# Linear attention and a gated feed-forward on one core: Silu as tanh and a product during the attention

## The chip, the cores and the metric

The kernel runs on one core of one Trainium2 chip. The metric is the time of one execution in microseconds (us) on the device. A core has TensorE (PE: matrix products and transposes, into the accumulator memory PSUM), VectorE (DVE), ScalarE (ACT: functions such as exp, and copies), GpSimd (POOL) and SyncE (SP, which here issues the DMAs). Each engine runs its own instructions in the order of its queue; semaphores order the engines among each other.

## The reference

Eight batches of eight heads, 576 tokens, head dimension 64, 128 random features, all in float32; then a gated feed-forward part on 4608 tokens of 512 numbers with 1536 hidden units.

```python
def phi(x):
    proj = einsum('bhsd,md->bhsm', x, omega)
    sq = sum(x * x, axis=-1, keepdims=True) / 2.0
    h = proj - sq
    h = h - max(h, axis=-1, keepdims=True)
    return exp(h) / sqrt(m)
q_p, k_p = phi(q * scale), phi(k * scale)
kv = einsum('bhsm,bhsd->bhmd', k_p, v)
z = sum(k_p, axis=2)
attn = einsum('bhsm,bhmd->bhsd', q_p, kv) / (einsum('bhsm,bhm->bhs', q_p, z)[..., None] + 1e-06)
x = attn.transpose(0, 2, 1, 3).reshape(4608, 512)
g = x @ w_gate
out = (g * (1.0 / (1.0 + exp(-g))) * (x @ w_val)) @ w_out
```

## The kernel before

Two streams of work share the engines for the first half of the time: the attention, and the feed-forward part of the tokens that are already through it.

**The attention** goes in steps. A step takes two groups of 256 tokens of a pair of heads, first keys alone, then a query and a key group each, at the end two query groups. For a step PE transposes q and k (the tile pt, copied to x by ACT, L454), PE projects them (pp, L469), DVE takes the maxima (L490) and forms the bias (L492, L493), and ACT takes Exp into ph (L505). POOL makes the squares (L446). The keys' ph go into the running sums kvacc on PE; ACT copies a finished sum out (kvr, L521). A query's ph is transposed on PE (ptq) and copied by ACT into a tile qt (`q_transpose`, L632 and L633). For the first four batches the quotient comes after the product with kv: PE makes po (`q_mult`), DVE divides (xn, L658), PE transposes xn (xt). For the later four the quotient comes first: POOL multiplies ph by the sums of the keys (jk, L563 and L567), DVE adds up and inverts (dj, L571 to L573), POOL scales ph (L583), and the matmuls of `q_out` make xt from qt and kvr. ACT copies xt into the resident tiles of the first three token tiles (L709, with DVE's L710 for the low part), or into xo, which a DMA stores for later (L703, L704).

**The feed-forward part.** Tokens come in nine tiles of 512, the hidden units in twelve blocks of 128. Each operand is split into a high and a low part, and a product is three matmuls. In the first round three token tiles (0 to 2) meet four sets of three blocks: twelve visits, in the generator `stream`. A visit makes for each block f of its set the gate g (twelve matmuls into one PSUM bank of the pool of three that `ps_moe` hands out), then Silu of each gate on ACT into the SBUF tile sl (L800), then the products of the visit before with w_out that are still due (`down`), then for each block the value v (twelve matmuls), h = v times sl on DVE (L820), and the split of h by ACT (L823) and POOL (L824). `down` adds its results up in acc, by ACT's copy the first time (L760), by DVE after that (L763). The weights are converted on the way by ACT, DVE and POOL (L289 to L303) and split by L263 and L264. In the second half, after the attention, the six other token tiles are taken in pairs by a scheme with seven products (`pair_rounds`), with a Silu of its own (L1038), which the change leaves alone.

**What orders the work.** The steps' functions are called in a written order (`CLOSE`, then `GROUPED`); between them the function `give` draws from `stream` as much matrix work as a plan of due times says. The framework then places the instructions of every engine from this order, their dependences and the free buffers. After the last step the attention's pools are closed (`late.close()`), and the dictionary `late_pools` gets the pools of the second half; until then it is empty. Eleven of the twelve visits have issued their Silus by then; the twelfth visit's three come after it. `att` is one of the attention's pools; with bufs=N a tile of a tag waits until the N-th one before it has been read for the last time.

Of the kernel before, what the change touches and what calls it, by code (L numbers as in the profile page):

```python
# [11 lines left out]
F32 = mybir.dt.float32  # L12
# [4 lines left out]
AF = mybir.ActivationFunctionType  # L17
ALU = mybir.AluOpType
# [6 lines left out]
def kernel(  # L25
# [11 lines left out]
    nc = tc.nc  # L37
# [4 lines left out]
    P = 128  # L42
# [5 lines left out]
    G = 256  # L48
    CH = G // P
    T = 512  # L50
# [40 lines left out]
    att = late.enter_context(tc.tile_pool(name="att", bufs=2))  # L91
# [14 lines left out]
    def transpose(*args, **kw):  # L106
        newest_pe[:] = [nc.tensor.transpose(*args, **kw)]  # L107
        return newest_pe[0]
# [10 lines left out]
    def ps_moe(name, shape):  # L119
        return ps_m.tile(shape, F32, name=name, tag="m")  # L120
# [21 lines left out]
    def slots(n, kind):  # L142

        if not 0 <= n < NS:
            return []
        return [(i, b, g, (kgroups if kd == "k" else qgroups)[g]) for i, (kd, b, g) in enumerate(steps[n]) if kd == kind]
# [25 lines left out]
    def mm1_us(w):  # L172
        return 3 * NC * (w / 2.4 + 13) * US
# [31 lines left out]
    for n in range(NN + 1):  # L205
        vi = 0
# [111 lines left out]
    def need(f, i):  # L318
        while (f, i) not in converted:
            tick()  # L320
# [4 lines left out]
    def load_weights(f, i):  # L325
        need(f, i)
        landing.append([LAND, f, i, fetch((f,), i)[0]])

    def land(upto=None):

        for t in landing:
            t[0] -= upto is None
        while landing and (landing[0][0] <= 0 or upto in [(f, i) for _, f, i, _ in landing]):
            _, f, i, raw = landing.pop(0)
            new_weights(f, i)
            with behind_step():
                split_piece(f, i, raw)

    def fetch(fs, i, spare=None):
        raws_ = []  # L340
        for f in fs:
            if spare is None:
                raw = moe.tile([P, DM], F32, name=f"wraw{f}_{i}", tag="wraw", bufs=3)
            else:
                raw = spare.tile([P, DM], F32, name=f"wspare{f}_{i}", tag="spare", bufs=2)
            nc.sync.dma_start(raw, wscr[f, i])
            raws_.append(raw)
        return raws_
# [270 lines left out]
    qts = {}  # L619
    xns = {}  # L620

    def q_transpose(n):
        m = n
        todo = [(b, g) for _, b, g, gr in slots(n - TLAG, "q") if b < BPOOL]
        todo += [(b, g) for _, b, g, gr in slots(n - NLAG, "q") if b >= BPOOL]
        for i, (b, g) in enumerate(todo):
            ph = box.pop(("q", b, g))
            pt = (ps_moe if m < EARLY else ps_tr if i else ps_att)(f"ptq{b}_{g}", [P, 2, G])
            for hh in range(2):
                for c in range(CH):  # L630
                    transpose(pt[:, hh, c * P : (c + 1) * P], ph[:, c, hh * M : (hh + 1) * M], ident)
            qts[b, g] = att.tile([P, 2, G], F32, name=f"qt{b}_{g}", tag="qt", bufs=4)  # L632
            nc.scalar.copy(qts[b, g], pt)  # L633

    def q_mult(n):
# [80 lines left out]
    def mm1(ps, wts, xs):  # L716

        wh, wl = wts
        xh, xl = xs
        n = 0  # L720
        for c in range(NC):
            ws = slice(c * P, (c + 1) * P)
            for a_, b_ in ((wh, xh), (wh, xl), (wl, xh)):
                matmul(ps, a_[:, ws], b_[:, c, :], start=n == 0, stop=n == 3 * NC - 1)
                n += 1
# [9 lines left out]
    def avail(j):  # L735
        return sum(TILES[j]) <= cols_done[0]
# [4 lines left out]
    def fetch_x(j):  # L741

        xt[j] = [xres.tile([P, NPAIR, T], F32R, name=f"x{e}{j}", tag=f"x{e}") for e in "hl"]
        for c in range(NC):
            raw = moe.tile([P, T], F32, name=f"xraw{j}_{c}", tag="wraw", bufs=3)
            nc.sync.dma_start(raw, x_dram[j][:, c, :])
            hi, lo = (t[:, c] for t in xt[j])
            nc.scalar.copy(hi, raw)
            nc.gpsimd.tensor_tensor(lo, raw, hi.bitcast(F32), op=ALU.subtract)

    def down(j, k_, ht, wts, next_set, tt):
        fs = sorted(ht)
        po = ps_moe(f"o{j}_{k_}_{tt}", [P, DM])
        for n, f in enumerate(fs):
            need(f, 2)
            land((f, 2))
            mm2(po, ht[f], weights[f, 2] if wts is None else wts[f], tt, n == 0, n == len(fs) - 1)
        if k_ == 0:
            acc[j, tt] = accp.tile([P, DM], F32, name=f"acc{j}_{tt}", tag="acc")
            nc.scalar.copy(acc[j, tt], po)  # L760
        else:
            a_ = acc[j, tt]
            nc.vector.tensor_tensor(a_, po, a_, op=ALU.add)  # L763
        if k_ == (NPF if j in paired else NSET) - 1:
            a_ = acc.pop((j, tt))
            for o in range(0, P, RES):
                nc.sync.dma_start(rows_of(TILES[j][0] + tt * P + o), a_[o : o + RES, :])
        if next_set is not None and tt == TILES[j][1] // P - 1:
            for f in next_set:
                load_weights(f, 2)  # L770

    def stream():

        todo = []
        for vi, (j, s_, k_) in enumerate(visits):
            nxt = visits[vi + 1] if vi + 1 < len(visits) else None
            new_set = nxt and nxt[1] != s_
            final = nxt is None
            w = TILES[j][1]
            while not avail(j):  # L780
                if todo:
                    down(*todo.pop(0))
                    yield MM2
                else:
                    yield None
            if j not in xt:
                fetch_x(j)
            xs = [t[:, :, 0:w] for t in xt[j]]
            fs = range(s_ * FA, (s_ + 1) * FA)
            pg, ht = {}, {}  # L790
            for f in fs:
                need(f, 0)
                land((f, 0))
                pg[f] = ps_moe(f"g{vi}_{f}", [P, T])[:, 0:w]
                mm1(pg[f], weights[f, 0], xs)
                yield mm1_us(w)

            for f in fs:
                sl = moe.tile([P, T], F32, name=f"sl{vi}_{f}", tag="sl", bufs=FA)[:, 0:w]
                nc.scalar.activation(sl, pg[f], AF.Silu)  # L800
                pg[f] = sl
            if new_set:
                for f in fs:
                    load_weights(nxt[1] * FA + f - fs[0], 0)
            if final:
                make_seven((0, 0), 0, fetch((0, 1), 0))
            while todo:
                down(*todo.pop(0))
                yield MM2

            if nxt and nxt[0] not in xt and avail(nxt[0]) and last_visit[nxt[0] - NXB] < vi:
                fetch_x(nxt[0])
            for f in fs:
                need(f, 1)
                land((f, 1))
                pv = ps_moe(f"v{vi}_{f}", [P, T])[:, 0:w]
                mm1(pv, weights[f, 1], xs)
                yield mm1_us(w)
                h = pg[f]
                nc.vector.tensor_tensor(h, pv, h, op=ALU.mult)  # L820
                hh = moe.tile([P, T], F32R, name=f"hh{vi}_{f}", tag="hh", bufs=FA)[:, 0:w]
                hl = moe.tile([P, T], F32R, name=f"hl{vi}_{f}", tag="hl", bufs=FA)[:, 0:w]
                nc.scalar.copy(hh, h)  # L823
                nc.gpsimd.tensor_tensor(hl, h, hh.bitcast(F32), op=ALU.subtract)  # L824
                ht[f] = hh, hl
                if new_set:
                    load_weights(nxt[1] * FA + f - fs[0], 1)
            if final:
                make_seven((0, 0), 1, fetch((0, 1), 1))
            for f in fs if vi else ():  # L830
                land((f, 2))
            wts = {f: weights[f, 2] for f in fs} if vi else None
            then = range(nxt[1] * FA, nxt[1] * FA + FA) if new_set else None
            todo = [(j, k_, ht, wts, then, tt) for tt in range(w // P)]
        yield from pair_rounds(todo)
# [22 lines left out]
    late_pools = {}  # L858
# [95 lines left out]
    def make_seven(key, i, raws_):  # L954
        for _ in seven_steps(key, i, raws_):
            pass
# [16 lines left out]
    def pair_rounds(todo):  # L973
# [121 lines left out]
        while one_down():  # L1095
            yield MM2

    ma = stream()
    debt = [0.0]
    given = [0.0]  # L1100
# [19 lines left out]
    def turn_next(n):  # L1120
# [8 lines left out]
        st_max,  # L1129
        lambda n: q_mult(n - 1),  # L1130
        q_transpose,
        lambda n: k_accumulate(n, 1),
        st_exp,
# [5 lines left out]
        q_out,  # L1139
        st_project,  # L1140
        q_transpose,
        lambda n: k_accumulate(n, 0),
        lambda n: k_accumulate(n, 1),
# [101 lines left out]
```

## Time and profile before

| | us |
|---|---|
| runs shown (three): median | 1165.86 |
| lowest, highest | 1165.11, 1166.25 |
| profiled execution, its own time | 1166.82 |
| span of its instructions | 1165.0 |

The profile is of one execution. Its views: busy time of each engine in chosen stretches; waits (who waited for whom: total, times, longest); groups of instructions by line, engine and shape (count, busy time, mean ns of one, idle time of the engine before them and what ended it); the chain of work that ended last, followed back from the last instruction; the instructions in order of time. "out<-in" names the tiles written and read, without buffer numbers. PEld is the loading of the stationary operand, which runs beside the matmuls. L103 and L107 are the lines of the helpers that issue all matmuls and transposes, so PE's work is told apart by its tiles: g, v and o (gate, value and output of the feed-forward part), pt, pp, ptq, po, xt, kvacc and zp (attention). Matmuls overlap in the pipeline, and their ends are modelled, so the mean duration of one says little; idle time of PE is what can be read.

### The profile page before, as it was taken

The numbers are of one execution on the slowest core, as the hardware profiler recorded it, in microseconds if no ns is written. First come the engines' busy times: TensorE is split into PE (matmuls) and PEld (weight loads), VectorE is DVE, ScalarE is ACT, GpSimd is POOL, SyncE is SP. The second block draws the span as 40 slices with busy tenths as digits, with TensorE's granted clock in tenths as the row PEclk, the third lists the DMA queues.
The fourth block names the chain that finished last, engine by engine and source line by source line (L and its number), as shares of the span: only waits on it lengthen the run. The fifth ranks groups of instructions, "written<-read, shape, count | busy, mean of one in ns | idle before, by whom it ended". The sixth has DMA issues, their size and how long they took to land.

```text
span 1165.0 us, 18915 instructions
## 1 busy us (share of the span) xinstructions
PE 1137.2 (98%) x6645; PEld 939.5 (81%) x6646; DVE 707.4 (61%) x1289; ACT 678.3 (58%) x1539; POOL 615.5 (53%) x559
## 2 busy tenths in 40 slices
PE   8999999999999999989999999999999999999998
PEld 6888888888878778867788778888878888888886
DVE  5787667455656656565474566665566666456654
ACT  5887886876776866757434544454544445444441
POOL 5664433344556675587245555544455543455551
PEclk9999999999999999999999999999999999999999
DMA  6764445655445642322544111124211111211103
GB/s 137 179 160 114 128 142 161 178 135 143 122 126 137 168 132 78 114 68 65 154 118 126 46 55 55 55 74 122 59 55 55 54 37 46 81 55 55 46 19 72
DMA packets 173966, 114.30 MB, mean 98 GB/s; under 512 B 125840, under 2 KB 144304, under 8 KB 173872
## 3 DMA queue, kind: packets, MB, share of 16 engines
q1 hardware_dynamic: 172528, 112.78, 35.5%
q8 instruction: 52, 0.85, 0.3%
q10 hardware_dynamic: 1344, 0.33, 0.1%
q14 instruction: 42, 0.34, 0.1%
HBM read 87.88 MB, written 25.18 MB: 97 GB/s over the span
## 4 chain that ended last, share of the span: by engine, by line
PE 74%; DVE 10%; ACT 6%; POOL 4%; DMA 3%; issue 2%; SPq 1%; ACTq 0%; POOLq 0%; DVEq 0%
PE o L103 22%; PE a L103 16%; PE c L103 8%; PE g L103 6%; PE pp L103 4%; PE v L103 4%; PE d L103 4%; PE kvacc L103 3%; ACT ph L505 3%; PE ptq L107 2%; PE po L103 2%; PE pt L107 2%; PE xt L103 1%; DVE st L490 1%; POOL wlo L264 1%
## 5 line engine op out<-in xcount | busy, mean ns | idle before, releaser
L505 ACT ACTIVATE ph<-pp,st 128x128 f32<-128x128 f32 x576 | 157.8, 386 | 26.5 <-DVE st L493 26.0
L763 DVE TENSOR_TENSOR acc<-o,acc 128x512 f32<-128x512 f32 x156 | 105.8, 684 | 94.6 <-PE o L103 94.3
L446 POOL TENSOR_TENSOR sq<-nat 128x512 f32<-128x512 f32 x72 | 78.2, 1086 | 130.5 <-DVE st L483 89.1
L950 POOL TENSOR_TENSOR wlo<-wspare,whi 128x512 fp32r<-128x512 f32 (+1 forms) x60 | 61.0, 1037 | 117.4 <-ACT whi L949 111.0
L490 DVE TENSOR_REDUCE st<-pp 128x4 f32<-128x512 f32 x144 | 92.5, 683 | 39.0 <-PE pp L103 38.7
L264 POOL TENSOR_TENSOR wlo<-wraw,whi 128x512 fp32r<-128x512 f32 x59 | 82.7, 1406 | 26.7 <-ACT whi L263 22.8
L103 PE MATMUL pp<-omT,x 64*128 64x128 f32 x1152 | 87.3, 285 | 3.2 <-ACT x L454 2.2
L103 PEld LDWEIGHTS pp<-omT,x 64*128 64x128 f32 x1152 | 72.6, 187 | 20.2 <-issue 11.2
L950 POOL TENSOR_TENSOR wlo<-s,whi 128x512 fp32r<-128x512 f32 x64 | 82.6, 1311 | 3.8 <-ACT whi L949 3.8
L1059 ACT COPY late<-a 128x512 f32<-128x512 f32 x72 | 42.2, 586 | 59.7 <-PE a L103 58.5
L103 PE MATMUL o<-whi,late 128*128 128x512 f32 x192 | 74.5, 389 | 0.0
L571 DVE TENSOR_REDUCE dj<-jk 128x4 f32<-128x512 f32 x36 | 24.6, 684 | 73.5 <-POOL jk L567 60.6
L103 PE MATMUL kvacc<-v,ph 128*128 128x65 f32 x512 | 65.9, 268 | 0.5 <-ACT kvr L521 0.5
L824 POOL TENSOR_TENSOR hl<-sl,hh 128x512 fp32r<-128x512 f32 x36 | 47.0, 1308 | 34.8 <-ACT hh L823 34.7
L103 PEld LDWEIGHTS kvacc<-v,ph 128*128 128x128 f32 x512 | 63.1, 192 | 0.8 <-ACT kvr L521 0.6
L1063 DVE TENSOR_TENSOR late<-c,late 128x512 f32<-128x512 f32 x25 | 17.3, 692 | 69.7 <-PE c L103 60.6
L103 PE MATMUL g<-xh,whi 128*128 128x512 f32 x144 | 59.4, 412 | 0.0
L103 PE MATMUL o<-whi,hh 128*128 128x512 f32 x144 | 58.5, 406 | 0.1
L303 POOL TENSOR_TENSOR wc<-st 128x512 int32<-128x512 int32 x36 | 37.5, 1042 | 39.6 <-DVE st L298 17.2
L103 PE MATMUL v<-xh,whi 128*128 128x512 f32 x144 | 57.9, 402 | 0.0
L103 PE MATMUL g<-xh,wlo 128*128 128x512 f32 x144 | 57.7, 401 | 0.0
L103 PE MATMUL g<-xl,whi 128*128 128x512 f32 x144 | 57.2, 397 | 0.0
(261 smaller groups left out, 3369.4 us busy)
## 6 DMA issues: line engine op xcount, KB each, us to landing
wraw<-wscr SPq DMA_DIRECT2D x63, 256.0 KB, 2.7
wspare<-wscr SPq DMA_DIRECT2D x60, 256.0 KB, 2.8
wscr<-wc SPq DMA_DIRECT2D x36, 256.0 KB, 2.2
out_dram<-acc SPq DMA_DIRECT2D x72, 128.0 KB, 2.4
nat<-in_k_dram SPq DMA_DIRECT2D x64, 128.0 KB, 3.0
nat<-in_q_dram SPq DMA_DIRECT2D x64, 128.0 KB, 3.1
v<-in_v_dram SPq DMA_DIRECT2D x62, 128.0 KB, 3.5
st<-in_moe_w_gate_dram SPq DMA_DIRECT2D x12, 512.0 KB, 4.1
```

Of the source, the lines that this page charges most:

```text
L103: newest_pe[:] = [nc.tensor.matmul(*args, **kw)]
L107: newest_pe[:] = [nc.tensor.transpose(*args, **kw)]
L264: nc.gpsimd.tensor_tensor(lo, raw, hi.bitcast(F32), op=ALU.subtract)
L303: nc.gpsimd.tensor_tensor(ui, ri, low, op=ALU.add)
L446: nc.gpsimd.tensor_tensor(sq, nat, nat, op=ALU.mult)
L490: nc.vector.tensor_reduce(st[:, 1, :, :, hh], pp[hh], axis=AX.X, op=ALU.max, negate=True)
L505: step_end["s"] = nc.scalar.activation(ph[:, c, hh * M : (hh + 1) * M], pp[hh][:, i, c, :], AF.Exp, bias=st[:, 3, i, c, hh : hh + 1], scal ...
L571: nc.vector.tensor_reduce(dn[:, 0], jk, axis=AX.X, op=ALU.add)
L763: nc.vector.tensor_tensor(a_, po, a_, op=ALU.add)
L824: nc.gpsimd.tensor_tensor(hl, h, hh.bitcast(F32), op=ALU.subtract)
L950: nc.gpsimd.tensor_tensor(lo, src_, hi.bitcast(F32), op=ALU.subtract)
L1059: newest["s"] = nc.scalar.copy(keep[name], ps)
```

## The change

For the visits whose Silu is issued while `late_pools` is empty, ACT's Silu is replaced by three instructions. Since silu(g) = g / (1 + exp(-g)) = (tanh(g/2) + 1) times g/2, ACT writes tanh(g/2) into sl and g/2 into a new tile gs, both out of PSUM, and DVE forms (sl + 1) times gs in one instruction, from SBUF into sl. The tile gs is 128 by 512 float32 and has a single buffer in the attention's pool. The tiles qt, of the same size, have three buffers there and no longer four. The rest of the visit reads sl as before.

```diff
@@ -629,7 +629,7 @@
-            qts[b, g] = att.tile([P, 2, G], F32, name=f"qt{b}_{g}", tag="qt", bufs=4)
+            qts[b, g] = att.tile([P, 2, G], F32, name=f"qt{b}_{g}", tag="qt", bufs=3)
             nc.scalar.copy(qts[b, g], pt)
@@ -797,7 +797,13 @@
             for f in fs:
                 sl = moe.tile([P, T], F32, name=f"sl{vi}_{f}", tag="sl", bufs=FA)[:, 0:w]
-                nc.scalar.activation(sl, pg[f], AF.Silu)
+                if late_pools:
+                    nc.scalar.activation(sl, pg[f], AF.Silu)
+                else:
+                    gs = att.tile([P, T], F32, name=f"gs{vi}_{f}", tag="gs", bufs=1)
+                    nc.scalar.activation(sl, pg[f], AF.Tanh, scale=0.5)
+                    nc.scalar.mul(gs, pg[f], 0.5)
+                    nc.vector.scalar_tensor_tensor(sl, sl, 1.0, gs, op0=ALU.add, op1=ALU.mult)
                 pg[f] = sl
```

## The prediction, made before the changed kernel had run

> **What bounds the kernel now.** I read the page first, then busy time by stretches, then the waits of TensorE in the stretch that the change touches, then the chain and the order of time around its waits, and last the groups of ScalarE and VectorE.
>
> ```profile
> span 1165.0 us, 18915 instructions
> PE 1137.2 (98%) x6645; PEld 939.5 (81%) x6646; DVE 707.4 (61%) x1289; ACT 678.3 (58%) x1539; POOL 615.5 (53%) x559
> PEclk9999999999999999999999999999999999999999
> ```
>
> TensorE is busy almost throughout, at the full granted clock. The next view cuts the span: the attention with the first round of the feed-forward part (120 to 570 us), the passage to the second part, and the second part.
>
> ```profile
> 120.00:300.00 180.00, 176.97 (x1251) 149.50 (x1250) 106.23 (x232) 140.24 (x327) 79.19 (x68) 1.00 0.53 149
> 300.00:570.00 270.00, 260.74 (x1741) 206.07 (x1740) 156.04 (x321) 183.38 (x451) 173.62 (x156) 0.99 0.41 111
> 570.00:600.00 30.00, 30.00 (x133) 24.49 (x131) 26.86 (x38) 14.06 (x25) 9.23 (x7) 1.00 0.49 142
> 600.00:1165.00 565.00, 559.04 (x2459) 460.68 (x2457) 331.31 (x461) 250.84 (x448) 286.87 (x230) 1.00 0.22 64
> ```
>
> The columns after the length are PE, PEld, DVE, ACT, POOL. In 120 to 570 us PE idles 180 - 176.97 + 270 - 260.74 = 12.3 us, though ACT is busy 140.24 + 183.38 = 323.6 us of 450 (72%) and DVE 262.3 us (58%). So ACT is the fullest of the helpers, but what it can give back is bounded by those 12.3 us. This is who ends them:
>
> ```profile
> PE ptq L107 <- ACT xo L703: 2.9, 4, 2.1
> PE xt L107 <- DVE xn L658: 2.3, 2, 1.2
> PE zp L107 <- ACT kvr L521: 2.0, 3, 1.1
> PE pt L107 <- ACT qt L633: 1.9, 1, 1.9
> PE pp L103 <- ACT ph L505: 1.0, 2, 0.8
> PE pt L107 <- ACT xo L703: 0.7, 2, 0.4
> PE xt L103 <- ACT x L454: 0.7, 1, 0.7
> PE ptq L107 <- issue: 0.4, 1, 0.4
> PE pt L107 <- DVE xl L710: 0.2, 1, 0.2
> ```
>
> ACT ends 2.9 + 2.0 + 1.9 + 1.0 + 0.7 + 0.7 = 9.2 us of it, DVE 2.5 us.
>
> **ScalarE: what goes and what comes.** These groups are of 120 to 570 us (busy, mean ns, idle time before):
>
> ```profile
> L505 ACT ACT_TABLE_LOAD x20 | 25.7, 1283 | 0.4
> L800 ACT ACT_TABLE_LOAD x21 | 26.9, 1283 | 2.2 <-PE g L103 1.9
> L800 ACT ACTIVATE sl<-g 128x512 f32<-128x512 f32 x33 | 19.6, 601 | 4.4 <-PE g L103 4.2
> L633 ACT COPY qt<-ptq 128x512 f32<-128x512 f32 x54 | 31.3, 591 | 21.0 <-PE ptq L107 21.0
> ```
>
> Silu (L800) and Exp (L505) take turns, and each turn costs a table load: 41 in all. The 33 Silus of this stretch are those of the first eleven visits, issued while the attention's pools are open; they become Tanh. The twelfth visit's three run later and stay Silu, so one load must come before the first of them. If Tanh needs no table but Exp's, 41 - 1 = 40 loads go: 40 x 1.283 = 51.3 us of ACT. No row here has a Tanh. [...] A Tanh of this shape is priced as the Silu it replaces, 0.60 us, so that exchange is free. The added copy of g/2 reads one PSUM bank as L633 does: 33 x 0.60 = 19.8 us. ACT's net is -51.3 + 19.8 = -31.5 us, 10% of its 323.6 us.
>
> [...]
>
> The load that stays comes before the twelfth visit's first Silu. There it is covered: in 570 to 600 us PE is busy for all 30.00 us while ACT has 14.06 us of work. If that cover were gone it would cost 1.3 us.
>
> **How much of that reaches TensorE.** Near a wait, the chain of waits and the order of time show what was late:
>
> ```profile
> 383.61 1.28 ACT L800
> 384.89 0.01 issue
> 384.90 0.42 ACT sl L800
> 385.32 0.08 issue
> 385.39 0.58 ACT qt L633
> 385.98 0.29 ACT kvr L521
> ```
>
> ```profile
> 386.31 0.27 PE L107 MATMUL zp<-ident,kvr 128*4 128x128 f32 x1 [0.59 <-ACT kvr L521]
> ...
> 519.91 1.28 ACT L800 ACT_TABLE_LOAD   x1
> 521.20 0.60 ACT L800 ACTIVATE sl<-g 128x512 f32<-128x512 f32 x1
> ...
> 522.21 1.17 PE L107 MATMUL ptq<-ident,ph 128*128 128x128 f32 x8 [0.18 <-ACT xo L703]
> ...
> 531.78 0.41 PE L107 MATMUL ptq<-ident,ph 128*128 128x128 f32 x2 [0.43 <-issue]
> ```
>
> A load stands right ahead of the copy that PE waits for at 386.31 (0.59 us), 522.21 (0.18) and, by ACT's place in time, 531.78 (0.43): 1.2 us together. The other waits are of another kind, the largest ones too:
>
> ```profile
> 514.04 0.62 ACT L823 CAST hh<-sl 128x512 fp32r<-128x512 f32 x1 [1.94 <-DVE sl L820]
> ACT qt L633 <- PE ptq L107: 21.0, 28, 1.3
> ```
>
> At 514.04 ACT itself stood idle, its cast queued ahead of the qt copies and waiting for DVE; the 1.9 us of "pt <- ACT qt" follow from that, and no load is in it. And 28 times ACT reached the qt copy before PE had made its input: mostly PE leads and ACT follows with time to spare, which is why 51 us of loads leave only 1.2 us of visible idling. Of the remaining 9.2 - 1.2 = 8.0 us I take the share by which ACT gets emptier, 10%: 0.8 us. Term: -2.0 us; bounds 0 (other waits come last) and -9.2 us (all of ACT's).
>
> **VectorE: the product.** One scalar_tensor_tensor from two SBUF tiles, 33 times. The nearest row is L298, the same operation and size in int32 (first min/median/max over the run, then the mean in the stretch):
>
> ```profile
> L298 DVE SCALAR_TENSOR_TENSOR st<-st,wc x36: 676/689/1658, 40.4 to 485.3; 128x512 int32<-128x512 int32 x36
> L298 DVE SCALAR_TENSOR_TENSOR st<-st,wc 128x512 int32<-128x512 int32 x31 | 27.2, 876 | 0.7
> L446 POOL TENSOR_TENSOR sq<-nat x72: 1039/1042/1422, 6.2 to 517.3; 128x512 f32<-128x512 f32 x72
> ```
>
> I take the mean, since the product runs among the same neighbours: 33 x 0.876 = 28.9 us, 11% more than DVE's 262.3 us; the bounds are 33 x 0.676 = 22.3 and 33 x 1.658 = 54.7 us. Queued behind it on DVE are the two maxima of the projections and the statistics (Exp waits for these), xn (PE's transposes wait), the running sums and h = v times silu (the casts wait). PE's idling on DVE is 2.5 us now. Scaled by 11% that grows by 0.3 us; one more wait of the kind "xt <- xn" costs 1.2 us; one for each of the eleven visits would cost 13 us. No fewer waits than now can come of it alone, so the lower end is 0. I take +0.8 us, between the first two.
>
> **The single buffer of g/2.** The second and third copy of a visit overwrite the tile that the product before must have read, so a new wait of ACT on DVE comes in.
>
> ```profile
> 208.87 0.60 ACT L800 ACTIVATE sl<-g 128x512 f32<-128x512 f32 x1
> ...
> 210.13 0.60 ACT L800 ACTIVATE sl<-g 128x512 f32<-128x512 f32 x1 [0.67 <-PE g L103]
> ```
>
> With two gates this close, Tanh and copy end 1.2 us after the first start, the product 0.7 to 1.7 us later, and the second Tanh takes 0.6 of that: the second copy waits 0.1 to 1.1 us. Over 22 such copies that is 2.2 to 24 us of ACT, less than the 31.5 us freed; so I cost it at 0 on PE. If DVE is itself held up, the cover is gone (rival B). Each gate's PSUM bank comes free after 1.2 us of ACT work rather than 1.28 + 0.60 = 1.9 us (with a load) or 0.6 us (without). No PE wait above names the gate's Silu, so I count nothing either way.
>
> **Three buffers for qt.** In the steps with two queries the third buffer and the first serve the next step, and the first was read by that step's opening matmuls, which TensorE's order puts ahead of the transposes that feed the copy. Cost 0; where it fails, the qt copy waits one projection (some 1 us), and the qt rows would name PE xt or po.
>
> **Sum.** -2.0 + 0.8 + 0 + 0 = -1.2 us. The profiled execution took 1166.82 us (span 1165.0 and 1.8 around it), 0.96 us above the median of 1165.86. So the forecast is 1165.86 - 1.2 = 1164.7 us. About 0.2% (2.3 us) is what a measurement of this kernel can tell from no change: I forecast none that can be told.
>
> **Rivals.** *A, faster.* ACT's emptier queue also ends the waits that have no load in them, because every exp and copy comes some 1.3 us sooner: two thirds of 9.2 us go, 6.1, less 0.8 for DVE: 1160.6 us. For it: ACT ends three quarters of PE's idling. Against it: the row of 514.04.
>
> *B, slower.* The product sits on DVE behind an instruction that waits for POOL, the copy of g/2 sits on ACT behind the product, and exp, x and qt copies sit behind that copy. Place: 300 to 570 us, where these rows come from:
>
> ```profile
> DVE dj L571 <- POOL jk L567: 60.6, 28, 4.2
> DVE dj L571 <- POOL jk L563: 12.9, 4, 5.6
> ```
>
> Each such wait is 73.5 / 32 = 2.3 us, up to 5.6. If four of the dozen second and third copies there meet one, and PE loses 1.6 us each (2.3 less the 21.0 / 28 = 0.7 us by which ACT otherwise waits for PE), that is +6.4, and -1.2 + 6.4 = +5.2: 1171.1 us. It decides from 3.5 us of new PE idling on. Against it: DVE is idle 42% of the stretch, so most products start at once.
>
> *C, the port.* L298's spread (689 to 1658 ns) and L446's (1042 to 1422) show DVE and POOL instructions lengthened at times. If each product also held POOL for its length, POOL would lose 33 x 0.689 = 22.7 us on the path jk, dj, statistics, Exp, and "pp <- ACT ph" (1.0 us) might treble: +2.0, in all +0.8: 1166.7 us. [...]
>
> *D, it does not do what it says.* Tanh gets a set of its own, and 41 loads stay: ACT +19.8 us (6%), so 0.6 us more idling on it, and 0.8 for DVE: 1167.3 us.
>
> **How the numbers follow.** Forecast 0.36, A 0.30, B 0.25, C 0.06, D 0.03. The forecast's own range is 1162.5 to 1168.5; a share of 0.05 of it lies below 1163.5. Faster: 0.30 + 0.05 = 0.35. Slower, above 1168.2: B and 0.03 from the tails of the forecast, C and D, 0.28. Between: 0.37. The range reaches from just beyond A, 1159.5, to about B's centre, 1171.0.
>
> **What would show it.** One load before the last visit's Silu and one at the start, no others; Tanh and copy at 0.60 us each; product near 0.88; ACT in 120 to 570 us down by some 31 us, DVE up by 29; PE's idling there 11 us against 12.3. Wrong would be: loads at Tanh (D), ACT rows of the g/2 copy waiting for the product with PE idle behind them (B), waits of PE on ACT under 4 us (A), or POOL's means up (C).

## The result, and the profile after

| | before | after |
|---|---|---|
| median, us | 1166.05 | 1173.9 |
| lowest to highest | 1165.11 to 1167.19 (6 runs) | 1172.93 to 1175.07 (5 runs) |
| profiled execution, its own time | 1166.82 | 1173.89 |
| span | 1165.0 | 1172.1 |

The change makes the kernel slower: the ratio is 1.0063, 95% interval 1.0053 to 1.0074. The forecast, no change that can be told, was wrong, and the time lies above its range. (A sixth execution of the changed kernel took 6396.4 us; it is left out everywhere.)

The page of the kernel after, first lines:

```profile
span 1172.1 us, 18949 instructions
PE 1141.3 (97%) x6646; PEld 943.7 (81%) x6646; DVE 733.5 (63%) x1322; ACT 644.0 (55%) x1532; POOL 620.8 (53%) x559
PEclk9999999999999999999999999999999999999999
```

TensorE is idle for 1172.1 - 1141.3 = 30.8 us against 27.8 before, and *busy* for 4.1 us longer with the same matmuls. So the 7.1 us of span fall into 3.0 of waiting and 4.1 of longer busy time. The same stretches as in the prediction (after the length: PE, PEld, DVE, ACT, POOL; then the granted clock):

```profile
120.00:300.00 180.00, 177.73 (x1257) 150.40 (x1256) 115.85 (x246) 125.28 (x324) 80.86 (x68) 1.00 0.54 149
300.00:570.00 270.00, 258.80 (x1724) 205.44 (x1723) 170.13 (x338) 160.47 (x441) 175.37 (x155) 0.98 0.40 110
570.00:600.00 30.00, 29.58 (x131) 24.18 (x130) 20.99 (x31) 14.87 (x26) 5.80 (x5) 1.00 0.42 123
600.00:1165.00 565.00, 561.78 (x2465) 462.97 (x2464) 336.60 (x468) 253.84 (x454) 291.88 (x234) 1.00 0.22 63
```

In 120 to 570 us ACT is busy 285.75 us, 37.9 less than before, and DVE 285.98, 23.7 more. The exchange took place roughly as planned (31 less and 29 more were forecast; 31 of the 33 products fall into the stretch), and yet PE idles 2.27 + 11.20 = 13.5 us there, not 12.3. The waits of PE in that stretch, the largest:

```profile
PE ptq L107 <- POOL wlo L264: 3.2, 1, 3.2
PE pp L103 <- ACT ph L505: 2.2, 3, 1.4
PE pt L107 <- ACT qt L633: 1.9, 1, 1.9
PE kvacc L103 <- ACT kvr L521: 1.4, 1, 1.4
...
PE xt L107 <- DVE xn L658: 0.2, 1, 0.2
```

Some waits shrank ("xt <- xn" was 2.3), others are new. Three places carry the loss.

**Place 1, 532 to 535 us.** The order of time, all engines:

```profile
531.71 2.94 POOL L264 TENSOR_TENSOR wlo<-wraw,whi 128x512 fp32r<-128x512 f32 x2
531.91 1.61 DVE L806 SCALAR_TENSOR_TENSOR sl<-sl,gs 128x512 f32<-128x512 f32 x1
533.56 0.60 ACT L805 ACTIVATE gs<-g 128x512 f32<-128x512 f32 x1 [1.85 <-DVE sl L806]
534.05 0.70 ACT L703 COPY xo<-xt 128x256 f32<-128x256 f32 x3
...
534.85 1.06 PE L107 MATMUL ptq<-ident,ph 128*128 128x128 f32 x8 [3.24 <-POOL wlo L264]
```

The product runs beside a POOL instruction and takes 1.61 us; ACT's copy of the next g/2 stands 1.85 us waiting for it, because gs has one buffer; the copy of xt out of PSUM is queued behind that copy; PE waits for it. The row names POOL, but POOL's wlo goes to the feed-forward part; the copies of xt end at 534.05 + 0.70 = 534.75 us, and PE starts 0.10 us later. In the kernel before they ended at 531.67 and PE started at 531.78, while POOL's wlo ran on to 533.16; PE waited 0.43 us at this transpose.

**Place 2, 301 to 303 us.** DVE makes a product first and the maxima behind it; Exp, and PE behind Exp, wait for them:

```profile
298.70 0.66 DVE L806 SCALAR_TENSOR_TENSOR sl<-sl,gs 128x512 f32<-128x512 f32 x1
299.28 1.28 DVE L490 TENSOR_REDUCE st<-pp 128x4 f32<-128x512 f32 x2
...
301.00 2.18 ACT L505 ACTIVATE ph<-pp,st 128x128 f32<-128x128 f32 x8 [2.44 <-DVE st L493]
302.71 1.91 PE L103 MATMUL pp<-omT,x 64*128 64x128 f32 x16 [1.44 <-ACT ph L505]
```

In the kernel before the maxima start at 298.80, a table load on ACT ends at 300.65, and Exp starts at 300.66. So the load is gone here, and Exp is no sooner. The pause is also longer because TensorE has another order: before, a group of transposes (ptq, 0.66 us) stood between xt and pp, and now it stands behind pp.

**Place 3, the twelfth visit,** whose Silus the change leaves alone:

```profile
598.41 0.60 ACT L801 ACTIVATE sl<-g 128x512 f32<-128x512 f32 x1
598.90 0.62 ACT L955 CAST whi<-wraw 128x512 fp32r<-128x512 f32 x1
...
602.71 0.62 ACT L955 CAST whi<-s 128x512 fp32r<-128x512 f32 x1 [2.15 <-DVE s L941]
603.24 0.59 ACT L801 ACTIVATE sl<-g 128x512 f32<-128x512 f32 x1
603.88 0.50 PE L103 MATMUL o<-whi,hh 128*128 128x512 f32 x1 [1.97 <-ACT sl L801]
604.93 0.63 PE L103 MATMUL o<-whi,hh 128*128 128x512 f32 x1
```

The framework now puts the visit's third Silu behind the casts of the first weights of the second half. They wait for DVE, and PE waits with them. In the kernel before the three Silus ran by 597 us.

**The clock.** The last row shows why busy time grew: the matmul takes 0.63 us; the same one took 0.39 at 601.07. The starts of such matmuls lie 0.43 us apart there and 0.23 at 601. In stretches of 20 us, and in the one of 3 us around that row, the kernel after:

```profile
300.00:320.00 20.00, 18.53 (x113) 15.18 (x111) 11.85 (x27) 9.84 (x28) 7.96 (x8) 0.83 0.40 111
520.00:540.00 20.00, 16.49 (x116) 13.01 (x117) 14.51 (x26) 13.44 (x37) 15.27 (x13) 0.91 0.25 66
600.00:620.00 20.00, 18.03 (x73) 14.46 (x72) 11.50 (x16) 6.84 (x13) 11.59 (x10) 0.91 0.57 168
604.50:607.50 3.00, 3.00 (x9) 2.35 (x8) 3.00 (x5) 0.14 (x1) 1.60 (x2) 0.50 0.10 38
```

The granted clock was 0.83, 0.91 and 0.91 in the stretches of 20 us, and 0.50 around the slow matmul: 20 x (0.17 + 0.09 + 0.09) = 7.0 us of full speed lost, right behind the three places. Up to its last matmul the kernel before has one such stretch, 0.91 in 420 to 440 us, 1.8 us. The difference of 5.2 us is more than the growth of busy time. In steps of 0.2 us the clock of the kernel after reads 0.50 from 304.0 to 310.8, from 536.1 to 539.5 and from 604.4 to 607.8 us, so for 6.8, 3.4 and 3.4 us, and that of the kernel before from 425.2 to 428.6, for 3.4 us.

### The profile page after: what moved, and what is told of

The parts are those of the page before. It is cut to its first block, busy times and chain, and to the rows that moved or that the text cites. A ratio compares the mean times of both kernels' runs of the same rounds, so it can differ in the third digit from the quotient of the medians.

```text
span 1172.1 us, 18949 instructions
## 1 busy us (share of the span) xinstructions
PE 1141.3 (97%) x6646; PEld 943.7 (81%) x6646; DVE 733.5 (63%) x1322; ACT 644.0 (55%) x1532; POOL 620.8 (53%) x559
## 4 chain that ended last, share of the span: by engine, by line
PE 77%; DVE 11%; ACT 4%; POOL 3%; issue 2%; DMA 2%; SPq 1%; POOLq 0%; DVEq 0%; ACTq 0%
PE o L103 23%; PE a L103 16%; PE c L103 8%; PE g L103 6%; PE v L103 5%; PE pp L103 5%; PE d L103 4%; PE kvacc L103 4%; PE po L103 2%; PE ptq L107 2%; PE pt L107 2%; ACT ph L505 2%; DVE st L490 1%; PE xt L103 1%; POOL wlo L264 1%
## 5 line engine op out<-in xcount | busy, mean ns | idle before, releaser
L264 POOL TENSOR_TENSOR wlo<-wraw,whi 128x512 fp32r<-128x512 f32 x59 | 83.5, 1419 | 23.7 <-ACT whi L263 20.7
L103 PE MATMUL o<-wlo,hh 128*128 128x512 f32 x144 | 57.6, 400 | 0.0
L103 PE MATMUL o<-whi,hl 128*128 128x512 f32 x144 | 57.6, 400 | 0.0
```

The source lines that it names most:

```text
L103: newest_pe[:] = [nc.tensor.matmul(*args, **kw)]
```

## The experiments

All ratios are to the kernel before, run on the same chip (median there 1166.2 to 1167.1 us). Idle is span less PE's busy time in the profiled execution.

| kernel | median us | ratio | 95% interval | span | PE idle |
|---|---|---|---|---|---|
| e1_qt3 | 1166.31 | 0.9994 | 0.9985 to 1.0004 | 1165.4 | 27.8 |
| e2_tanh_only | 1159.01 | 0.9926 | 0.9910 to 0.9943 | 1157.2 | 22.5 |
| e3_added_only | 1179.78 | 1.0110 | 1.0094 to 1.0125 | 1177.5 | 35.3 |
| e4_from_psum | 1163.16 | 0.9965 | 0.9952 to 0.9978 | 1161.9 | 25.6 |
| f1_last_order | 1170.29 | 1.0026 | 1.0015 to 1.0038 | 1164.7 | 28.8 |
| f2_gs_bf16x2 | 1169.79 | 1.0027 | 1.0017 to 1.0037 | 1169.2 | 29.1 |
| f3_tanh_copy | 1164.44 | 0.9979 | 0.9968 to 0.9989 | 1163.4 | 26.6 |
| f4_tanh_product | 1171.61 | 1.0039 | 1.0025 to 1.0053 | 1171.5 | 31.9 |
| g1_psum_order | 1161.43 | 0.9953 | 0.9940 to 0.9965 | 1159.6 | 24.9 |
| g2_both | 1167.53 | 1.0009 | 1.0000 to 1.0018 | 1164.0 | 28.0 |
| g3_all_twelve | 1161.00 | 0.9952 | 0.9939 to 0.9964 | 1159.6 | 23.4 |
| g4_tanh_product_order | 1168.16 | 1.0021 | 1.0011 to 1.0031 | 1165.4 | 27.4 |

**e1_qt3.** The kernel before with qt's three buffers alone.

```diff
-            qts[b, g] = att.tile([P, 2, G], F32, name=f"qt{b}_{g}", tag="qt", bufs=4)
+            qts[b, g] = att.tile([P, 2, G], F32, name=f"qt{b}_{g}", tag="qt", bufs=3)
```

> The kernel before with three buffers for qt instead of four, nothing else. Coupling theory (the loss comes of waits that the added instructions make: ScalarE waits for the product through the single tile gs, the statistics queue behind the product, and each TensorE pause that follows pulls the granted clock to half for 3.4 us): same as before, 1166 us within 1, one half-clock stretch. Rival, buffer theory (the missing qt buffer delays the copies and re-places the queues): a good part of the loss is here, 1169 to 1174 us.

0.9994, the interval holds 1. The missing buffer costs nothing, as forecast. The half clock for 3.4 us is what three of the four stretches above show, the fourth has 6.8 us; that each pause brings one was a theory, and the profiled run of f1 below does not bear it out.

**e2_tanh_only.** The loads removed, nothing added; qt keeps four buffers.

```diff
-                    gs = att.tile([P, T], F32, name=f"gs{vi}_{f}", tag="gs", bufs=1)
                     nc.scalar.activation(sl, pg[f], AF.Tanh, scale=0.5)
-                    nc.scalar.mul(gs, pg[f], 0.5)
-                    nc.vector.scalar_tensor_tensor(sl, sl, 1.0, gs, op0=ALU.add, op1=ALU.mult)
```

> Tanh in place of Silu in the eleven visits, without the copy of g/2 and without the product (the output lacks the factor; four qt buffers). It shows what the table loads are worth alone. Coupling theory: 1 to 4 us faster than before, 1162 to 1165 us, VectorE as before. Rival, order theory (whatever moves ScalarE's times makes the framework place the queues anew, and the new placement loses by itself, above all the last visit's third Silu that now comes 6 us later behind the casts of the next weights): 1168 us or more, with the same pause near 603 us.

0.9926, 8.6 us less, more than either reading had expected; the output lacks the factor g/2. Its windows and all its waits of PE over 0.5 us in 120 to 570 us:

```profile
120.00:300.00 180.00, 178.77 (x1263) 150.71 (x1261) 104.47 (x235) 119.74 (x317) 80.73 (x70) 1.00 0.55 152
300.00:570.00 270.00, 264.88 (x1765) 210.81 (x1766) 160.92 (x329) 154.89 (x426) 172.26 (x154) 0.99 0.41 117
```

```profile
PE pt L107 <- ACT qt L633: 1.9, 1, 1.9
PE ptq L107 <- ACT xo L703: 1.4, 2, 1.0
PE zp L107 <- ACT kvr L521: 1.1, 1, 1.1
PE pt L107 <- ACT xo L703: 0.7, 2, 0.4
PE pp L103 <- ACT ph L505: 0.7, 2, 0.4
```

PE's idling there falls from 12.3 to 1.23 + 5.12 = 6.4 us. ACT's waits go from 9.2 to 5.8, and DVE's from 2.5 to 0.4: part of what was booked on DVE ended too when ACT had less to do. Busy time falls by 2.5 us as well. The one wait that was traced to a stall and not to a load, "pt <- qt" of 1.9 us, is still there to the digit.

TensorE's order belongs to this gain. The traces of all kernels without the loads, from e2 to the kernel after, hold the matmuls and transposes in one and the same order. It differs from the order of the kernel before (which e1 shares), as at place 2, and e3 has a third one. So the 8.6 us are the loads and the new order together, and no run parts them.

**e3_added_only.** The other half alone: Silu and its loads stay, copy, product and three qt buffers are added.

```diff
-                    nc.scalar.activation(sl, pg[f], AF.Tanh, scale=0.5)
+                    nc.scalar.activation(sl, pg[f], AF.Silu)
```

> Silu stays, with its table loads; the copy of g/2, the product and three qt buffers are added as in the change (the output is then (silu+1)*g/2 through the rest). Coupling theory: slower than the changed kernel or equal, 1173 to 1180 us, with waits of ScalarE's copy for the product of 7 us or more and two or more half-clock stretches. Order theory: less than the changed kernel, 1166 to 1171 us, since the loads keep the old places.

1.0110, within the range expected: with no relief, copy and product cost 12.8 us, PE's idling 7.5 us of it. That is not a clean price: PE idles 3.74 us in 570 to 620 us against 0.13 before, so the twelfth visit is disturbed here too.

**e4_from_psum.** The product reads g where it is, in PSUM, so that no copy and no gs is needed; the half goes into the product with v; qt keeps four buffers.

```diff
-                    gs = att.tile([P, T], F32, name=f"gs{vi}_{f}", tag="gs", bufs=1)
                     nc.scalar.activation(sl, pg[f], AF.Tanh, scale=0.5)
-                    nc.scalar.mul(gs, pg[f], 0.5)
-                    nc.vector.scalar_tensor_tensor(sl, sl, 1.0, gs, op0=ALU.add, op1=ALU.mult)
+                    nc.vector.scalar_tensor_tensor(sl, sl, 1.0, pg[f], op0=ALU.add, op1=ALU.mult)
...
-                nc.vector.tensor_tensor(h, pv, h, op=ALU.mult)
+                if vi < len(visits) - 1:
+                    nc.vector.scalar_tensor_tensor(h, pv, 0.5, h, op0=ALU.mult, op1=ALU.mult)
+                else:
+                    nc.vector.tensor_tensor(h, pv, h, op=ALU.mult)
```

> Tanh as in the change, but VectorE forms (tanh+1)*g straight out of PSUM, with no copy and no tile gs, and the half goes into the product with v (one instruction as before); four qt buffers. ScalarE loses all 51 us of loads, VectorE gets the same 33 products with one SBUF input. Coupling theory: 1161 to 1166 us, products near 0.69 us with no 1.6 us ones. Order theory: 1170 us or more like the changed kernel. A risk for both: the gate's bank now waits for VectorE.

0.9965: faster than the kernel before. The product's row, durations min/median/max:

```profile
L804 DVE SCALAR_TENSOR_TENSOR sl<-sl,g x33: 655/676/690, 125.1 to 566.4; 128x512 f32<-128x512 f32 x33
```

Not one of the 33 is lengthened. In the kernel after, the same instruction with both inputs in SBUF:

```profile
L806 DVE SCALAR_TENSOR_TENSOR sl<-sl,gs x33: 660/693/1752, 127.2 to 573.9; 128x512 f32<-128x512 f32 x33
```

**f1_last_order.** After, with the weights of the second half issued behind the third Silu; PE's order is the same as after.

```diff
-                    nc.scalar.activation(sl, pg[f], AF.Silu)
+                    last_silu = nc.scalar.activation(sl, pg[f], AF.Silu)
...
-                make_seven((0, 0), 0, fetch((0, 1), 0))
+                with tc.issue_after(last_silu.ins):
+                    make_seven((0, 0), 0, fetch((0, 1), 0))
```

> The changed kernel with one edge of order more: the casts of the pair weights in the twelfth visit queue behind that visit's third Silu on ScalarE; the other engines keep the changed kernel's order of TensorE. Theory of the pauses (of the 7 to 8 us lost, some 4 come from the pause near 602 us: 2.0 + 0.4 us of TensorE idling and 1.7 us by the half clock after it): 1169 to 1171 us, no half-clock stretch near 604 us. Rival (the pause is covered by other slack, or the casts then come late instead): 1173 to 1175 us as the changed kernel.

1.0026 against 1.0063, as expected: place 3 is worth 4.3 us. Its ten executions also part the clock from the waits. The profiled one took 1166.49 us with a mean granted clock of 1.000; the other nine, of the same program, had 0.994 to 0.997 and took 1169.0 to 1171.66. In the profiled one the pauses of places 1 and 2 are there and the drops of the clock are not:

```profile
300.00:320.00 20.00, 18.52 (x126) 15.00 (x123) 14.18 (x29) 12.61 (x37) 10.52 (x9) 1.00 0.40 109
...
520.00:540.00 20.00, 16.78 (x125) 12.77 (x123) 14.72 (x30) 11.97 (x35) 14.70 (x12) 1.00 0.26 74
```

So in that execution the clock added nothing to the pauses; the other nine, at a lower mean clock, took some 4 us more by their median (1170.54). Where their clock fell is not known, since only the one execution was traced.

**f2_gs_bf16x2.** After, with g/2 in two buffers (as bf16, so that the two take the room of the one float32 tile).

```diff
-                    gs = att.tile([P, T], F32, name=f"gs{vi}_{f}", tag="gs", bufs=1)
+                    gs = att.tile([P, T], BF16, name=f"gs{vi}_{f}", tag="gs", bufs=2)
```

> The changed kernel with gs as two bfloat16 tiles in the room of the one float32 tile (g/2 is rounded); TensorE's and GpSimd's order is the changed kernel's, on ScalarE and VectorE a few neighbours change places. Coupling through the single tile: ScalarE's copy no longer waits for the product (7.5 us in the changed kernel), the 3.2 us pause near 531 us and its half-clock stretch go, 1167 to 1170 us. Rival (the product's load on VectorE does it, not the buffer): 1172 to 1175 us.

1.0027: 4.2 us less than after. The row "ACT gs <- DVE sl" (7.5 us in after) is gone. At place 1 ACT no longer waits, and PE waits 1.25 us there instead of 3.24:

```profile
531.42 0.68 ACT L805 ACTIVATE gs<-g 128x512 bf16<-128x512 f32 x1
531.89 0.80 ACT L703 COPY xo<-xt 128x256 f32<-128x256 f32 x3
...
532.79 1.06 PE L107 MATMUL ptq<-ident,ph 128*128 128x128 f32 x8 [1.25 <-issue]
```

xt is copied out 2.2 us sooner than in after (534.05). The edit changes the type too, but the products are no shorter for it: 0.91 us in the mean of all 33 against 0.88.

**f3_tanh_copy and f4_tanh_product.** Tanh with the copy but no product; Tanh with the product but no copy (its second input a constant tile in SBUF).

```diff
-                    nc.vector.scalar_tensor_tensor(sl, sl, 1.0, gs, op0=ALU.add, op1=ALU.mult)
```

```diff
+    half = att.tile([P, T], F32, name="half", tag="gs", bufs=1)
+    nc.vector.memset(half, 0.5)
...
-                    gs = att.tile([P, T], F32, name=f"gs{vi}_{f}", tag="gs", bufs=1)
...
-                    nc.scalar.mul(gs, pg[f], 0.5)
-                    nc.vector.scalar_tensor_tensor(sl, sl, 1.0, gs, op0=ALU.add, op1=ALU.mult)
+                    nc.vector.scalar_tensor_tensor(sl, sl, 1.0, half, op0=ALU.add, op1=ALU.mult)
```

> Tanh and the copy of g/2 on ScalarE, no product on VectorE (the output lacks it; three qt buffers). The copy's 19.8 us of ScalarE alone: if ScalarE's fill is what TensorE feels, 3 us of the 8 us that the loads' removal gave go back, 1161 to 1163 us; if only VectorE and the coupling hurt, 1158 to 1160 us as with Tanh alone.

> Tanh on ScalarE and the product on VectorE from SBUF, but with a constant tile in place of g/2, so without the copy and without a wait of ScalarE for VectorE (the output has the constant 0.5 for g/2; three qt buffers). [...] If VectorE's load is the cost: 1163 to 1166 us, like the product out of PSUM or up to 2 us above it; if it is the coupling of copy and product: 1158 to 1161 us.

0.9979 and 1.0039, both above every range expected: with the copy 2.4 of the 8.6 us are left, and the product from SBUF undoes the gain and more. But in both the third place is disturbed too (PE idle 2.75 and 3.73 us in 570 to 620 us, against 0.63 in e2), so neither is a clean price. Hence the last four.

**g1_psum_order, g2_both, g4_tanh_product_order, g3_all_twelve.** The edit of f1 put into e4, into f2 and into f4; and g1 with the twelfth visit as Tanh and product too:

```diff
-                if late_pools:
-                    last_silu = nc.scalar.activation(sl, pg[f], AF.Silu)
-                else:
-                    nc.scalar.activation(sl, pg[f], AF.Tanh, scale=0.5)
-                    nc.vector.scalar_tensor_tensor(sl, sl, 1.0, pg[f], op0=ALU.add, op1=ALU.mult)
+                last_silu = nc.scalar.activation(sl, pg[f], AF.Tanh, scale=0.5)
+                nc.vector.scalar_tensor_tensor(sl, sl, 1.0, pg[f], op0=ALU.add, op1=ALU.mult)
...
-                if vi < len(visits) - 1:
-                    nc.vector.scalar_tensor_tensor(h, pv, 0.5, h, op0=ALU.mult, op1=ALU.mult)
-                else:
-                    nc.vector.tensor_tensor(h, pv, h, op=ALU.mult)
+                nc.vector.scalar_tensor_tensor(h, pv, 0.5, h, op0=ALU.mult, op1=ALU.mult)
```

> The version with the product out of PSUM (e4_from_psum: Tanh, then (tanh+1) times g with g read from PSUM, the half in the product with v, no copy, no gs, qt with four buffers), and in addition the pair weights of the second half issued after the third Silu of the twelfth visit, as in f1_last_order. In e4_from_psum PE idles 1.71 us in 570 to 620 us; with the edge in place f1 had 0.61 there. If the last visit's order is a cost of its own, it goes here too: 1.1 us less idling, so 1162.0 us against e4's 1163.16, 0.9955 of the kernel before, and below it by more than a measurement can tell. If the order cost something only together with a half-clock stretch (e4's records have little of it), nothing changes: 1163.2 us.

> The change with both mends: g/2 in two bf16 tiles (f2_gs_bf16x2, -4 us) and the order of the last visit (f1_last_order, -4 us). If the single buffer and the last visit are two separate places of loss, the two add up: 1174.1 - 4 - 4 = 1166 us, level with the kernel before (0.999 to 1.001), and what is left between this and e2_tanh_only (1159.0) is the price of copy and product, some 7 us. If both only shift pauses about, so that the one mend takes what the other would have taken, it stays near 1170 us (1.0025 to 1.003).

> Tanh and the product from two SBUF tiles, the second one constant at 0.5, no copy of g/2 (f4_tanh_product, 1171.6 us; its output lacks the factor g), with the last visit's order mended. Against g1_psum_order it differs in where the product's second input lies (SBUF or PSUM) and in the half in the product with v. If f4's excess over e4_from_psum (8.4 us) was the operand in SBUF (products of 0.945 us in the mean against 0.676, and longer POOL instructions beside them), it stays above g1 by 5 us or more: 1167 us or above. If it was f4's order in the last visit, it falls to g1's time within 2 us: 1162 to 1164 us.

> As g1_psum_order, with the twelfth visit as Tanh and product too, so that the load for Silu comes with the first pair round and no longer at 595 us. That load is covered in 570 to 600 us, where PE in the kernel before is busy throughout; then nothing is gained: 1162 us as g1. If the load ahead of the last Silus is itself what delays the casts behind them, one load (1.3 us) goes from PE's idling there: 1160.7 us. If three more products on DVE in the passage delay the casts of the pair weights, it is 1 to 2 us slower than g1.

g1, 1161.43 us, is 4.8 us faster than the kernel before; its gain over e4 (1.4 us by the ratios) lies within the intervals. g3 equals g1: the load that stays costs nothing, as the prediction's cover said. g2 is level with the kernel before, between its two expectations: the two mends give 6.3 us together, not 4.3 + 4.2. g4 against g1, with the same order of TensorE's work, settles where the product's input should lie in this kernel. The product and POOL's L583 in g1, in 120 to 570 us:

```profile
L804 DVE SCALAR_TENSOR_TENSOR sl<-sl,g 128x512 f32<-128x512 f32 x33 | 22.0, 677 | 14.2 <-ACT sl L803 14.2
L583 POOL TENSOR_TENSOR ph<-ph,dj 128x512 f32<-128x512 f32 x36 | 38.2, 1064 | 20.9 <-DVE dj L573 17.9 <-DVE dj L572 1.0 <-PE pp L103 0.8
```

And in g4 (its lines stand two further down):

```profile
L806 DVE SCALAR_TENSOR_TENSOR sl<-sl,half 128x512 f32<-128x512 f32 x33 | 30.9, 946 | 14.7 <-ACT sl L805 14.7
L585 POOL TENSOR_TENSOR ph<-ph,dj 128x512 f32<-128x512 f32 x36 | 40.2, 1119 | 20.9 <-DVE dj L575 17.9 <-PE pp L105 1.2 <-DVE dj L574 1.0
```

With the operand in SBUF both are longer in the mean, DVE's product by 40% (946 against 677 ns) and POOL's instruction by 5% (1119 against 1064 ns), and the time is 6.7 us longer (1168.16 against 1161.43).

## Why the prediction was wrong

The kernels make a ladder from the loads' gain to the result; each step is a difference of ratios times 1166 us:

| step | from, to | us |
|---|---|---|
| loads gone, and TensorE's new order | before, e2 | -8.6 |
| product, g from PSUM (with f1's edge) | e2, g1 | +3.1 |
| its second input in SBUF | g1, g4 | +7.9 |
| copy of g/2 into two buffers of bf16 | g4, g2 | -1.4 (within the intervals) |
| one buffer of float32 for the two of bf16 | g2, f1 | +2.0 |
| order of the last visit | f1, after | +4.3 |
| sum | before, after | +7.3 |

Point by point:

- **Loads and prices: right.** One load is left at the start (1.28 us, at 3.33) and one ahead of the twelfth visit (1.28 us, at 595.59). Tanh and copy took 0.63 us each (forecast 0.60), the product 0.89 (0.88). So Tanh needs no load beside Exp in this kernel: the 33 Tanhs and 576 Exps have none among them after the one at the start. The 40 loads of the sum rested on this as an assumption of the author's, which no run had shown by then; rival D is out. Groups of after in 120 to 570 us, the last two columns busy and mean ns, then idle:

```profile
L805 ACT ACTIVATE gs<-g 128x512 f32<-128x512 f32 x31 | 19.7, 635 | 7.6 <-DVE sl L806 7.5
L804 ACT ACTIVATE sl<-g 128x512 f32<-128x512 f32 x31 | 19.6, 632 | 7.7 <-PE g L103 7.6
L806 DVE SCALAR_TENSOR_TENSOR sl<-sl,gs 128x512 f32<-128x512 f32 x31 | 27.7, 894 | 17.2 <-ACT gs L805 17.0
```

- **"Term: -2.0 us": failed in size.** Without the loads, and in TensorE's new order, e2 gained 8.6 us. The step "a load stands right ahead of the copy that PE waits for" counted only loads that touch a wait, in an order that it took as fixed. In e2 waits booked on DVE ended too (2.5 to 0.4 us), and busy time fell by 2.5 us, which the sum did not have. Rival A's 6.1 us was nearer, and even that was short.
- **"I take +0.8 us, between the first two" for VectorE, and "I cost it at 0 on PE" for the buffer: these failed and decide the sign.** By the ladder product, copy and buffer cost 3.1 + 7.9 - 1.4 + 2.0 = 11.6 us (e3, with a disturbed twelfth visit, 12.8), and with the order of the last visit they took back nearly twice what e2 gained. DVE's busy time over the span rose nearly as forecast, by 26.1 us of 28.9; the mistake was to turn a busy share into idling of PE in proportion. The case put aside there, one more wait for each visit, 13 us, comes near in size by luck: the rows show a few long pauses and a lower clock, not a wait in each visit.
- **"If DVE is itself held up, the cover is gone (rival B)": right in part, at place 1.** The rows of 532 to 535 us hold B's chain from the copy of g/2 on. Its first link is another: DVE was making dj (0.65, 0.63 and 0.18 us in a row from 530.46), not waiting for POOL, when the product came due, and the product itself was lengthened (1.61 us; the median of the 33 is 0.693). ACT's copies waited four times for the product (0.29, 2.08, 3.28 and 1.85 us, 7.5 together), but only the last reached PE; behind the two long ones, at 399 and 444 us, PE was busy throughout (8.00 of 8 us in 396 to 404, 10.00 of 10 in 440 to 450).
- **Rival C ("the port") had a chance of 0.06, and the operand in SBUF is the largest single cost,** 6.7 to 7.9 us by g1 against g4. The prediction looked for it in POOL's lost time alone; the larger lengthening is in the product itself (0.677 us in the mean in g1, 0.946 in g4), and the statistics are queued behind it. ACT's waits for them in 120 to 570 us rose from 10.8 to 21.1 us, but the operand in SBUF is the smaller part of that: e2, with no product, has 14.2, g1, with products that are not lengthened, 19.3, and g4 22.7. The longest product took 0.690 us with one input in PSUM (e4) and 1.752 us with two in SBUF (after). That each product holds POOL for its length, 22.7 us in all, was the author's assumption, and no run shows it: POOL's groups in 120 to 570 us come to 255.3 us in g1 and 258.2 us in g4, with one instruction of 1.1 us fewer. By what mechanism the two engines' instructions get longer, no run shows either.
- **Not in the sum: the order of the last visit,** 4.3 us. It is not a cost of the new instructions but of where the framework puts unchanged ones once the times around them shift.
- **Not in the sum: the clock.** In the profiled executions it is 5.2 us of the 7.1 us of span. It isn't a step of its own in the ladder, as the low stretches there stand right behind the three pauses.
- **Three buffers for qt: right,** 0 (e1).

What stays open: how much of e2's gain is the loads and how much TensorE's new order; why the clock drops behind some pauses and not behind others of the same length; by which path the SBUF operand's cost reaches PE (in the profiled executions g4 has 2.5 us more idling and 3.3 us more busy time than g1), and how it divides into the longer products and POOL's longer instructions (g1 and g4 differ also in the half in the product with v, and in qt's buffers, which e1 shows to cost nothing); and why the mends of f1 and f2 don't add up in full. The steps from e2 to g1 and from g2 to f1 lie close to their intervals.

## What to carry to other kernels

An engine that is 58 to 72% busy (DVE and ACT before, in 120 to 570 us) can still be late at the few places where PE depends on it; price an added instruction by what is queued behind it there (here some 12 us for 33 products and copies), not by its share of the busy time. Where the data of a two-input VectorE instruction lie in PSUM anyway, try it with that input read from there: here this saved the copy, the buffer and 6.7 us, and made of a loss of 7.3 us a gain of 4.1 by the ratio (e4), with no mend of the order. When a change shifts the times, read the order of the unchanged instructions next to it as well.

## What the runs showed of the hardware that was not expected

The granted clock of a PE that is 97% busy fell to half (0.50 in 604.5 to 607.5 us) behind pauses of 1.4 to 3.2 us: behind places 1 to 3 matmuls of 0.39 us took 0.63. In the profiled execution of f1 it did not fall at all behind two of the same pauses (1.42 and 3.22 us); the other nine executions of that program had lower mean clocks (0.994 to 0.997). In f2 it stayed at 1.00 in 600 to 620 us behind a pause of 2.12 us. So the length of a pause did not tell here whether the clock would fall: it fell behind 1.44 and 3.24 us in the kernel after, and not behind 1.42 and 3.22 us in f1. What lowers it, no run shows.
